# One-token attention from a key/value cache beside a small MLP: the unused matmuls of a step moved to its end and made 24, and the scores put behind all the transposes

## The chip, the cores and the metric

The kernel runs on one core of one Trainium2 chip. The metric is the device time in microseconds (us), taken as the median over several executions. Beside the times there is one profiled execution with its trace. A profile line names engines as PE (TensorE matmul), PEld (TensorE weight load), DVE (VectorE), ACT (ScalarE), POOL (GpSimd) and SP (SyncE, which issues the large transfers here).

## The reference

The inputs are bf16: two rows `x` of 512, key and value caches of shape 2 x 32 x 8192 x 128, and the weights of the projections and of the MLP.

```python
def _A_ref(x, k_cache, v_cache, wq, wo):      # H, Dh = 32, 128; Sq = 1
    q = (x @ wq).reshape(B, Sq, H, Dh).transpose(0, 2, 1, 3)
    scores = einsum("bhqd,bhkd->bhqk", q, k_cache) * (Dh ** -0.5)
    p = softmax(scores, axis=-1)
    o = einsum("bhqk,bhkd->bhqd", p, v_cache)
    return o.transpose(0, 2, 1, 3).reshape(B, Sq, H * Dh) @ wo

def _B_ref(x, w1, w2):
    return einsum("bsf,fd->bsd", maximum(einsum("bsd,df->bsf", x, w1), 0), w2)

xn = layernorm(x)
return x + _A_ref(xn, k_cache, v_cache, wq, wo) + _B_ref(xn, w1, w2)
```

There are 64 pairs of batch and head, and each has one query against 8192 keys. Every byte of the caches is read once and used once.

## The kernel before, in words

**Steps and tiles.** The 64 pairs are done four at a time (`U = 4`), so there are `NP = 16` steps. The keys of a step are one tile `ks` of 128 partitions by 32768 bf16: 32 partitions belong to one pair, and each partition holds 256 keys (`KB`) of 128 elements. The values of a step are a tile `vs` of the same form. There is one buffer of each: the next keys can be written over `ks` only when it has been read out, and the same holds for `vs`. The caches are 32 such tiles, which is 268 of the 280.5 MB that the profile counts as read.

**What TensorE does in a step.** The keys lie with the key number on the partitions, while the scores need the head's elements there. So the function `transposes(e)` (line 280) turns eight blocks of 128 x 128 through PSUM (`tp`, four buffers used in turn), and DVE or ACT copies each group of eight into one of 32 SBUF tiles `kT` (line 432, `kcopies`; twenty groups fall to DVE, twelve to ACT). `scores(e)` (line 287) multiplies the eight blocks of group `e` with the four queries `q4` into one PSUM area `Sc`. There are `NG = 32` groups. The first loop does `transposes(e)` and, from `e = LAG` on, `scores(e - LAG)` behind it; a second loop does the scores that are left. With `LAG = 28`, four score groups are mixed in: the order is T28 S0 T29 S1 T30 S2 T31 S3, then S4 to S31.

While the scores go on, DVE reduces them to a maximum (line 479), TensorE turns that (`turn`, line 299) and spreads it over the partitions (`spread`, line 305), and ACT takes the exponentials into `prm` (line 553). This is done for two halves of the scores. Then 256 matmuls of `vs` with `prm` (line 346) give the output `ot`; the last of them raises the semaphore `sW`.

**Unused matmuls.** At the head of each step stand `WARM = 16` matmuls of the identity with itself into the PSUM tile `ms` (line 313). Nobody reads their result. They wait for nothing. Behind them TensorE waits for the step's keys (`dK[0]`).

**Order of the transfers.** All large transfers are issued from SP's one queue, in a fixed order written by hand: keys of step 0, values of step 0, keys of step 1, values of step 1, and so on. Before it issues the keys of the next step, SP waits for the last transpose of this one (semaphore `pT[HG - 1]`); before it issues the next values it waits for `sW`:

```python
for t in range(NP):
    if t > 0:
        sp.wait_ge(pT[HG - 1], NH * t)
    load(ks, K_all, t, dK, 0 < t < NP - 1)
    if t == 0:
        sp.wait_ge(sQ, 2)
    else:
        sp.wait_ge(sW, t)
    load(vs, V_all, t, dV, t < NP - 1)
```

The first and the last step's keys and the last step's values are loaded in two halves with a semaphore each, the others whole. Ahead of the steps come the query projection (line 259); behind them the weights of the MLP and of the output projection are loaded over `ks` and used (lines 376 and 403). The output projection takes its weights in four pieces of 18, 8, 4 and 2 blocks.

**The loop on TensorE.** The steps are a run-time loop (`pe.Fori`), whose body is in the program once; a few registers (`reg`, `g`, `h`) hold the values that the semaphores are to reach and are advanced at its end. `reg` is 1 in the first step and 16 in the last.

Of the kernel before, what the change touches and what calls it, by code (L numbers as in the profile page):

```python
# [12 lines left out]
EG = 8  # L13
NG = 32
REP = 16
LAG = 28
TR = (21, 25)
BC = 32
WARM = 16
ON_ACT = (0, 3, 5)  # L20


# [1 line left out]
def kernel(  # L24
# [13 lines left out]
    P = 128  # L38
# [3 lines left out]

    Bsz, Sq, D = A_x.shape
    _, H, Sk, Dh = A_k_cache.shape
    Dff = B_w1.shape[1]
    assert Dh == P and D % P == 0 and Dff % P == 0 and Sk % HP == 0
# [4 lines left out]
    NP = N // U  # L51
# [17 lines left out]
    def sb(shape, dt, name):  # L69
        return ctx.enter_context(nc.sbuf_tensor(name, shape, dt))  # L70

    def ps(shape, dt, name):
        return ctx.enter_context(nc.psum_tensor(name, shape, dt))
# [14 lines left out]
    identb = sb([P, P], bf16, "identb")  # L88
# [41 lines left out]
    ms = ps([P, 512], f32, "ms")  # L130
# [80 lines left out]
    def advance(eng, regs):  # L211
        for r, step in zip(regs, (1, 2, 2) + (NH,) * NH):
            eng.reg_add(r, r, step)
# [35 lines left out]
    def _(pe):  # L249
        pe.wait_ge(sI, 1)  # L250
        pe.wait_ge(sV, 5)
        for kt in range(KT):
            i = pe.transpose(tpx[:, kt, :], xn[:, kt, :], identb[0:Bsz, 0:Bsz])
# [3 lines left out]
        for g in range(QG):  # L257
            for kt in range(KT):
                i = pe.matmul(  # L259
                    qp,  # L260
                    lhsT=xz[:, kt, Z - g * Bsz:Z - g * Bsz + QG * Bsz],
                    rhs=vs[:, (kt * QG + g) * 512:(kt * QG + g + 1) * 512],
                    start=(g == 0 and kt == 0),
                    stop=(g == QG - 1 and kt == KT - 1),
                )
        i.then_inc(sQ, 1)
        pe.wait_ge(sV, 7)
        for l in range(QH):
            i = pe.transpose(
                tpq[:, l, :], qs[:, l * Dh:(l + 1) * Dh], identb[0:QG * Bsz, 0:QG * Bsz]  # L270
            )
        i.then_inc(sQ, 1)

        def rep(ap, n):
            return ap.rearrange("p (o u) -> p o u", o=1).to_broadcast([P, n, U])

        def transposes(e):
            for i in range(EG):
                kk = e * EG + i
                t = pe.transpose(tp[e % 4][:, i, :], ks[:, kk * Dh:(kk + 1) * Dh], identb[:])  # L280
            t.then_inc(pT[e % HG], 1)

        def scores(e):
            for i in range(EG):
                kk = e * EG + i
                n = min(REP, BK - kk % BK)
                t = pe.matmul(  # L287
                    Sc[:, U * kk:U * (kk + n)],
                    lhsT=kT[e][:, i, :],
                    rhs=rep(q4[:], n),  # L290
                    start=True,
                    stop=True,
                )
            if e % (NG // 2) == NG // 2 - 1:
                t.then_inc(sS, 1)

        def turn(i):
            pe.wait_ge(sM, g[i])
            pe.transpose(  # L299
                trp[:, i * P:(i + 1) * P], mcol[:, i:i + 1], identb[:]  # L300
            ).then_inc(sT, 1)

        def spread(i):
            pe.wait_ge(sX, g[i])
            pe.matmul(  # L305
                bc[:, i, :], lhsT=onesb[:], rhs=mx[:, i, :], start=True, stop=True
            ).then_inc(sB, 1)

        regs = counters(pe, mybir.EngineType.PE)
        reg, g, h = regs[0], regs[1:3], regs[3:]  # L310
        with pe.Fori(16, NL + 1, 16) as n16:
            for i in range(WARM):
                pe.matmul(  # L313
                    ms[:], lhsT=identb[:],
                    rhs=identb[:].rearrange("p (o k) -> p o k", o=1).to_broadcast([P, 4, P]),
                    start=True, stop=True,
                )
            pe.wait_ge(dK[0], n16)
            pe.wait_ge(sQ1, reg)
            for e in range(NG):  # L320
                if e == NG // 2:
                    pe.wait_ge(dK[1], n16)
                if e >= 4:
                    pe.wait_ge(kR[(e - 4) % HG], h[(e - 4) // HG])
                transposes(e)
                if e >= LAG:
                    scores(e - LAG)
            for e in range(NG - LAG, NG):
                if e >= NG - 4:
                    pe.wait_ge(kR[e % HG], h[e // HG])  # L330
                scores(e)
                if e == TR[0]:
                    turn(0)
                if e == TR[1]:
                    spread(0)
            pe.wait_ge(sO, reg)
            for kk in range(KB):
                i, first = divmod(kk, KB // 2)
                if first == 0:
                    pe.wait_ge(sP, g[i])  # L340
                    if i == 0:
                        turn(1)
                    pe.wait_ge(dV[i], n16)
                if kk == BC:
                    spread(1)
                t = pe.matmul(  # L346
                    oh[:, i, :],
                    lhsT=vs[:, kk * Dh:(kk + 1) * Dh],
                    rhs=rep(prm[:, kk, :], REP),
                    start=(first == 0),  # L350
                    stop=(first == KB // 2 - 1),
                )
            t.then_inc(sW, 1)
            advance(pe, regs)

        pe.wait_ge(sI, 2 + U)
        dbp = Sc[:, 0:2 * N].rearrange("p (t u) -> p t u", u=U)
        for u in range(U):
            t = pe.matmul(  # L359
                dbp[:, :, u], lhsT=onesh[:, u, :], rhs=RS[:].rearrange("p i t -> p (i t)"),  # L360
                start=True, stop=True,
            )
        t.then_inc(sH, 1)
        for k in range(KT):
            pe.matmul(
                fin[:, k * Bsz:(k + 1) * Bsz],
                lhsT=xsb[:, k * P:(k + 1) * P],
                rhs=identb[0:Bsz, 0:Bsz],
                start=(k == 0),
                stop=False,  # L370
# [3 lines left out]
        for j in range(FJ):  # L374
            for kt in range(KT):
                i = pe.matmul(  # L376
                    hp[:, j, :],
                    lhsT=w1_v[:, kt, j, :],
                    rhs=xz[:, kt, Z:Z + Bsz],
                    start=(kt == 0),  # L380
                    stop=(kt == KT - 1),
                )
# [8 lines left out]
        for dq in range(DQ):  # L391
            t = pe.matmul(  # L392
                ox.rearrange("p (b j) -> p b j", b=Bsz),
                lhsT=sel[:, dq, :],
                rhs=Ob[:, :, dq * WJ:(dq + 1) * WJ],
                start=(dq == 0),
                stop=(dq == DQ - 1),
# [198 lines left out]
```

## Time and profile before

| | |
|---|---|
| median of 14 runs | 668.48 us |
| fastest and slowest of them | 663.64 and 676.11 us |
| the profiled execution, its own time | 673.97 us |
| its span, first to last instruction | 672.1 us |
| mean granted TensorE clock | 0.967 |
| PE, DVE, ACT busy | 587.2, 263.7 and 292.8 us |
| large transfers (SP's queue) | 280.50 MB, 97.6% of 16 engines' span |
| read from HBM | 417 GB/s over the span |

The profiled execution took 5.5 us more than the median, so it is one of the slower of its kind. The span leaves out 1.9 us of the execution's own time. "Busy" of PE counts overlapping pipelined matmuls and is no measure of how near it is to its peak. The row of the granted clock says what share of its full clock TensorE was given.

### The profile page before, as it was taken

The page shows a single profiled execution, that of the slowest core. Times are in us where ns is not written, and L with a number is a line of the kernel's source. Part 1 is how long each engine was busy: PE and PEld are TensorE (multiplying, and loading weights), DVE is VectorE, ACT ScalarE, POOL GpSimd, SP SyncE. Part 2 cuts the span into 40 slices and gives each one's busy share as a digit, 9 for nine tenths or more (in the row PEclk, how much of TensorE's full clock was granted, in tenths as well). Part 3 has the DMA queues.
Part 4 walks back from the last instruction along what each step waited for, and adds up shares of the span by engine and source line. Part 5 has one row for each costly group of instructions (what it writes and reads, how often), then busy time and mean ns, then how long its engine had stood idle before and what let it go on. Part 6 is the DMA issues. An engine that isn't in the chain of part 4 may idle for free.

```text
span 672.1 us, 27441 instructions
## 1 busy us (share of the span) xinstructions
PE 587.2 (87%) x12907; PEld 539.7 (80%) x12907; DVE 263.7 (39%) x503; ACT 292.8 (44%) x532; POOL 7.1 (1%) x30
## 2 busy tenths in 40 slices
PE   2986898979989998998989889897998979899997
PEld 0586787969878797987869688696987869698987
DVE  1350532607145160715417062260715317071721
ACT  1243543527244453725435363352636425373730
POOL 2000000000000000000000000000000000000000
PEclk9999999999889998999989989899989989999987
DMA  8999999999999999999999999999999999999995
GB/s 375 438 439 423 434 433 437 433 433 406 433 437 378 437 433 437 429 402 421 437 437 413 433 433 398 437 378 437 425 413 413 421 433 390 437 437 406 437 421 210
DMA packets 6079, 280.66 MB, mean 418 GB/s; under 512 B 690, under 2 KB 692, under 8 KB 948
## 3 DMA queue, kind: packets, MB, share of 16 engines
q1 hardware_dynamic: 6064, 280.50, 97.6%
q8 instruction: 8, 0.13, 0.1%
q14 instruction: 3, 0.02, 0.0%
q10 hardware_dynamic: 4, 0.00, 0.0%
HBM read 280.50 MB, written 0.00 MB: 417 GB/s over the span
## 4 chain that ended last, share of the span: by engine, by line
DMA 52%; PE 47%; DVE 1%; issue 0%; SPq 0%
DMA ks<-in_A_k_cache_dram 50%; PE tp L280 36%; PE Sc L287 4%; PE ot L346 3%; DMA vs<-in_A_wq_dram 2%; PE ot L259 1%; PE ms L313 1%; PE Sc L403 1%; PE ms L376 1%; DVE mcol L479 0%; PE Sc L359 0%; PE ms L299 0%; DVE qs L461 0%; PE ms L305 0%; PE ms L392 0%
## 5 line engine op out<-in xcount | busy, mean ns | idle before, releaser
L432 DVE COPY kT<-tp 128x1024 bf16<-128x1024 bf16 x320 | 211.1, 688 | 273.1 <-PE tp L280 267.4
L280 PE MATMUL tp<-identb,ks 128*128 128x128 bf16 x4096 | 248.7, 223 | 38.7 <-DMA ks<-in_A_k_cache_dram 38.7
L280 PEld LDWEIGHTS tp<-identb,ks 128*128 128x128 bf16 x4096 | 239.1, 100 | 46.1 <-DMA ks<-in_A_k_cache_dram 45.6
L432 ACT COPY kT<-tp 128x1024 bf16<-128x1024 bf16 x192 | 190.0, 1013 | 144.2 <-PE tp L280 142.1
L287 PE MATMUL Sc<-q,kT 128*128 128x64 bf16 (+8 forms) x4096 | 140.4, 191 | 2.1 <-issue 2.1
L346 PE MATMUL ot<-prm,vs 128*128 128x64 bf16 x4096 | 135.3, 195 | 4.3 <-issue 4.3
L346 PEld LDWEIGHTS ot<-prm,vs 128*128 128x128 bf16 x4096 | 131.2, 99 | 6.3 <-issue 4.5
L287 PEld LDWEIGHTS Sc<-q,kT 128*128 128x128 bf16 x4096 | 132.5, 97 | 3.5 <-issue 2.2
L553 ACT ACTIVATE prm<-Sc,nm 32x128 bf16<-32x128 f32 x128 | 69.0, 539 | 5.4
L479 DVE TENSOR_REDUCE mcol<-Sc 32x1 bf16<-32x128 f32 x128 | 37.1, 289 | 79.1 <-PE Sc L287 77.8
L548 ACT COPY nm<-ms 128x4 f32<-128x4 f32 x32 | 5.2, 163 | 134.7 <-PE ms L305 134.7
L313 PE MATMUL ms<-identb 128*128 128x512 bf16 x256 | 57.8, 379 | 0.6 <-issue 0.6
L313 PEld LDWEIGHTS ms<-identb 128*128 128x128 bf16 x256 | 23.9, 97 | 27.2 <-issue 0.6
L564 ACT COPY OTf<-ot 128x8 f32 x16 | 2.7, 166 | 75.8 <-PE ot L346 75.8
L553 ACT ACTIVATION_READ_ACCUMULATOR prm<-Sc,nm x128 | 32.1, 251 | 0.0
L299 PE MATMUL ms<-identb,mcol 128*1 128x128 bf16 x32 | 6.9, 217 | 22.1 <-DVE mcol L479 22.1
L432 ACT ACT_TABLE_LOAD x16 | 20.5, 1283 | 3.6 <-issue 3.6
L299 PEld LDWEIGHTS ms<-identb,mcol 128*1 128x1 bf16 x32 | 2.5, 79 | 23.9 <-issue 23.1
L259 PE MATMUL ot<-vs,xz 128*16 128x512 bf16 x32 | 9.1, 454 | 8.6 <-DMA vs<-in_A_wq_dram 8.6
L486 DVE TENSOR_REDUCE mx<-ms 1x4 bf16<-1x128 bf16 x32 | 8.9, 279 | 16.0 <-PE ms L299 16.0
L259 PEld LDWEIGHTS ot<-vs,xz 128*16 128x16 bf16 x32 | 3.3, 103 | 13.9 <-issue 11.4
L240 POOL COPY q<-qb 128x4 bf16<-128x4 bf16 x16 | 3.0, 188 | 603.6 <-PE Sc L287 555.6
(61 smaller groups left out, 46.9 us busy)
## 6 DMA issues: line engine op xcount, KB each, us to landing
ks<-in_A_k_cache_dram SPq DMA_DIRECT2D x4, 4096.0 KB, 22.7
vs<-in_A_v_cache_dram SPq DMA_DIRECT2D x2, 4096.0 KB, 21.6
vs<-in_A_wq_dram SPq DMA_DIRECT2D x1, 4096.0 KB, 12.1
ks<-in_B_w_dram SPq DMA_DIRECT2D x2, 1792.0 KB, 14.3
ks<-in_A_wo_dram SPq DMA_DIRECT2D x1, 2304.0 KB
ks<-in_A_wo_dram SPq DMA_DIRECT2D x1, 1024.0 KB, 23.3
ks<-in_A_wo_dram SPq DMA_DIRECT2D x1, 512.0 KB, 24.1
ks<-in_A_wo_dram SPq DMA_DIRECT2D x1, 256.0 KB, 24.2
```

The source lines that it names most:

```text
L259: i = pe.matmul(qp, lhsT=xz[:, kt, Z - g * Bsz:Z - g * Bsz + QG * Bsz], rhs=vs[:, (kt * QG + g) * 512:(kt * QG + g + 1) * 512], start=(g = ...
L280: t = pe.transpose(tp[e % 4][:, i, :], ks[:, kk * Dh:(kk + 1) * Dh], identb[:])
L287: t = pe.matmul(Sc[:, U * kk:U * (kk + n)], lhsT=kT[e][:, i, :], rhs=rep(q4[:], n), start=True, stop=True,)
L299: pe.transpose(trp[:, i * P:(i + 1) * P], mcol[:, i:i + 1], identb[:]).then_inc(sT, 1)
L313: pe.matmul(ms[:], lhsT=identb[:], rhs=identb[:].rearrange("p (o k) -> p o k", o=1).to_broadcast([P, 4, P]), start=True, stop=True,)
L346: t = pe.matmul(oh[:, i, :], lhsT=vs[:, kk * Dh:(kk + 1) * Dh], rhs=rep(prm[:, kk, :], REP), start=(first == 0), stop=(first == KB // 2 - 1),)
L376: i = pe.matmul(hp[:, j, :], lhsT=w1_v[:, kt, j, :], rhs=xz[:, kt, Z:Z + Bsz], start=(kt == 0), stop=(kt == KT - 1),)
L403: t = pe.matmul(fin[:, k * Bsz:(k + 1) * Bsz], lhsT=w[:, j, k * P:(k + 1) * P], rhs=x[:, j, :], start=False, stop=(last and k == KT - 1),)
L432: fn(kT[e][:], tp[e % 4][:]).then_inc(kR[e % HG], 1)
L479: m = v.tensor_reduce(out=mcol[own, i:i + 1], in_=S[own, i * KB // 2:(i + 1) * KB // 2, u], axis=AX.X, op=ALU.max,)
L486: v.tensor_reduce(out=mx[:, i, :], in_=trp[:, i * P:(i + 1) * P].rearrange("o (u m) -> o u m", u=U), axis=AX.X, op=ALU.max, negate=True,). ...
L553: x = a.activation(out=prm[own, k, u], in_=S[own, k, u], func=ACTF.Exp, bias=nm[own, i, u:u + 1], scale=1.0, accum_out=RS[own, i, bass.ds( ...
```

## The change

The 16 unused matmuls at the head of a step are taken out. At the end of the step, behind the last output matmul and its semaphore, stand 24 of them inside a branch on the register `reg`. The branch lets them run where `reg` is below 15, which is in the first fourteen steps; behind the last step but one and behind the last they are skipped. So none stands ahead of the first step, none ahead of the last, and 24 stand ahead of each of the others. `LAG` becomes 32: the first loop holds the 32 groups of transposes alone, and the second all 32 groups of scores.

```diff
-LAG = 28
+LAG = 32
 TR = (21, 25)
 BC = 32
-WARM = 16
+WARM = 24
...
         with pe.Fori(16, NL + 1, 16) as n16:
-            for i in range(WARM):
-                pe.matmul(
-                    ms[:], lhsT=identb[:],
-                    rhs=identb[:].rearrange("p (o k) -> p o k", o=1).to_broadcast([P, 4, P]),
-                    start=True, stop=True,
-                )
             pe.wait_ge(dK[0], n16)
             pe.wait_ge(sQ1, reg)
...
             t.then_inc(sW, 1)
+            with pe.If_lt(reg, NP - 1):
+                for i in range(WARM):
+                    pe.matmul(
+                        ms[:], lhsT=identb[:],
+                        rhs=identb[:].rearrange("p (o k) -> p o k", o=1).to_broadcast([P, 4, P]),
+                        start=True, stop=True,
+                    )
             advance(pe, regs)
```

## The prediction

> **What bounds the kernel now.** I read the page's busy slices first, then the DMA queue's own waits, the chain that ended last, and the timeline and stage windows around two neighbouring steps.
>
> ```profile
> PE   2986898979989998998989889897998979899997
> ...
> PEclk9999999999889998999989989899989989999987
> DMA  8999999999999999999999999999999999999995
> ...
> q1 hardware_dynamic: 6064, 280.50, 97.6%
> ...
> q8 instruction: 8, 0.13, 0.1%
> ```
>
> The transfers fill the span, so the time is 280.5 MB over the rate, plus whatever stops the transfers. PE's clock dips now and then. The queue's waits and the chain say what the transfers depend on:
>
> ```profile
> SPq L182 <- PE tp L280: 325.4, 15, 24.0
> SPq L182 <- PE ot L346: 262.6, 15, 23.7
> ...
> 87.85 23.45 DMA ks<-in_A_k_cache_dram
> ...
> 111.34 13.13 PE tp L280 x232
> ...
> 126.58 23.74 DMA ks<-in_A_k_cache_dram
> ...
> 150.37 14.75 PE tp L280 x232
> ...
> 167.23 24.63 DMA ks<-in_A_k_cache_dram
> ```
>
> The next keys (K) are issued when the last transpose is done; the values (V) of this step are then still landing. V's landing is its issue plus its time to landing in the DMA view: 104.97 + 25.7 = 130.7 us and 143.71 + 26.0 = 169.7. So in the first of these steps K is issued 126.58, which is 4.1 us ahead of V's landing, and lands 150.32 - 130.7 = 19.6 us after it. In the second it is issued at 167.23, only 2.5 us ahead, and lands 191.86 - 169.7 = 22.2 us after V. I did this for the thirteen whole K loads from 87.85 on. Seven leads are 4.0 to 4.4 us, with intervals 19.3, 19.6, 19.7, 19.3, 19.4, 20.0 and 20.5. Six are 2.4 to 2.8 us (issues at 167.2, 208.5, 364.2, 405.2, 445.8, 565.9), with intervals 22.2, 19.3, 21.7, 21.2, 20.9 and 20.4. A load without trouble takes 19.35 us. The late six cost 125.7 - 6 x 19.35 = 9.6 us, the other seven 137.8 - 7 x 19.35 = 2.4.
>
> ```profile
> vs<-in_A_v_cache_dram SPq DMA_DIRECT2D x1, 25.7
> ...
> vs<-in_A_v_cache_dram SPq DMA_DIRECT2D x1, 26.0
> ...
> 143.60:150.40 6.80, 3.62 (x20) 1.48 (x18) 0.00 (x0) 1.45 (x2) 0.00 (x0) 1.00 0.93 405
> 150.40:153.80 3.40, 3.40 (x33) 3.40 (x34) 1.36 (x2) 1.01 (x1) 0.00 (x0) 0.50 1.11 482
> ...
> 111.30:114.70 3.40, 3.36 (x61) 3.37 (x61) 2.00 (x4) 2.38 (x3) 0.00 (x0) 1.00 1.11 482
> ```
>
> These stage windows say why six were late (the third figure from the end is the clock). From V's issue to K's landing PE has 3.6 us of unused matmuls and then nothing; in the first 3.4 us of the transposes the clock is 0.50 with 33 matmuls, against 1.00 and 61 in the other step. The transposes then take 14.75 us instead of 13.13, and K's issue moves back by 1.6 us. The idle time before the transposes is 1.6 to 3.9 us over the steps; the cold starts follow 2.55 us and more, none a smaller one, though some gaps near 3 us stay warm.
>
> **The change, part by part.** The sum is made against the profiled execution's own 673.97 us (span 672.1 and 1.9 around it), which is 5.5 above the median.
>
> *24 instead of 16 unused matmuls, steps 1 to 14.* The 16 take 3.61 us, so one takes 3.61 / 16 = 0.22 and 24 take about 5.3. They start where they did: the end of a step and the head of the next are one stretch of PE's queue, behind the semaphore that releases V. From the last output matmul to K's landing there are 6.3 us in a usual step (104.97 to 111.29) and 4.7 to 5.1 where the output matmuls met a half clock (225.63 to 230.63). The gap shrinks from some 2.7 us to 1.0, and at its longest (541.63 to 549.02, 7.4 us) to 2.1, under the 2.55 from which I saw cold starts. In the short steps the block runs past K's landing by up to 0.6 us. It takes DVE, ACT and DMA nothing; what hides it is the wait for K, and where that cover is gone each us delays the transposes and K's issue one for one.
>
> *All scores behind all transposes.* Three score groups, 3 x 0.25 us in the chain, leave the stretch ahead of the last transpose: K's issue comes 0.75 us earlier, while the scores end as before and V's issue does not move. What has to keep up is the copy out of PSUM: DVE does five of each eight groups in 3.37 us and waits 0.20 for PE, so it follows at PE's pace for four more groups; the former breaks were spare. I cost it at 0, at most 0.2.
>
> Both together: the lead of K over V's landing is 4.1 + 0.75 = 4.85 us in a usual step and 4.85 - 0.6 = 4.25 where the block overruns. No step should be left at 2.4 to 2.8, so the 9.6 us go. The seven early steps' 2.4 us may go in part; I leave them in, and put them into the range.
>
> A rule of the Trainium skill speaks against putting every score behind the transposes. "TensorE: Matmul & The Clock Gate", Part 4, says that transposes do not count as busy work and that the full clock does not engage for them. By the rule the unbroken stretch would run at half the clock: 256 transposes in some 27 us instead of 14.4, an estimate, so about 12 us more per step. The row says otherwise: 232 unbroken transposes took 13.13 us, 57 ns each, at a clock of 1.00. I take the row.
>
> *None ahead of the first step.* The block there took 3.6 us of the chain at 23.86. The transposes start that much earlier, but K of step 1 was issued at 42.54, 10.6 us ahead of V's landing at 53.2. Worth 0; if the first transposes ran cold, the same lead covers it.
>
> *None ahead of the last step.* Here PE is the bound:
>
> ```profile
> 621.13 3.50 PE ms L313 x16
> 624.63 12.95 PE tp L280 x232
> ...
> 658.20 0.89 PE Sc L359 x8
> ...
> 663.83 5.02 PE Sc L403 x184
> ```
>
> All of PE behind it comes 3.5 us earlier. Two transfers can take that back. The last keys' second half lands near 628.3 (the two issues at 604.03 land after 19.2 us in the middle, 9.7 us apart); the first half of the transposes from 621.2 ends at 628.4, so it costs nothing. The last piece of the output weights, issued near 642.0, lands 24.2 later, at 666.2; eight matmuls at 5.02 / 184 = 27 ns follow, to 666.4, where the line now ends at 668.85. So 3.5 shrinks to 2.4 us.
>
> *The branch.* By the rows of the loop line, a branch of TensorE's sequencer takes 69 to 226 ns. Sixteen of them, each under 0.3 us, stand behind V's release and ahead of the unused matmuls or an empty wait: 0 in the middle. Skipped, one is on the path ahead of the last step and one behind it: at most 0.4 together. A rule speaks against it: "Runtime: NRT & Kernel Launch", Instruction fetch mechanics, says that a taken branch out of a two-page window makes the engine stall for a fetch. The trace has such stalls in the first pass of the body:
>
> ```profile
> 63.31 3.21 PE L346 MATMUL ot<-prm,vs 128*128 128x64 bf16 x101 [3.11 <-issue]
> ```
>
> They are 1.2 to 3.1 us each. By the rule the two taken skips cost up to 6.2 us, one of them on the path of the end, and the 2.4 would be gone. But every step already ends with a taken branch over the whole body, and the page has 8 instruction packets in all with no such stall after the first pass; a skip over 48 instructions is shorter. I take 0, and keep 3 for the range.
>
> Sum: 673.97 - 9.6 - 2.4 = 662.0. What is left holds no late K, so it should not depend on how many of them a run drew; against the median it is 6.5 lower. The fastest of the 14, 663.64, which can have had little of this loss, gives 663.64 - 2.4 = 661.2. I take 661.5, with 659 (the other 2.4 us gone too) to 664.5 (the fetch) as this case's own range.
>
> **Rivals.** *The late issue is not the cause* (the slow loads are the memory's doing, and the late transposes only stand beside them). For it: one late step, 208.5, lost nothing, and two early ones, 484.8 and 524.5, lost 0.7 and 1.1. Against: five of six late ones lost 1.0 to 2.8. Then the end's 2.4 us remain: 668.48 - 2.4 = 666.1, no change by the bound below.
>
> *The block becomes the bound ahead of the transposes,* the slower side. In steps with a half clock in the output matmuls the 24 already overrun; if the half clock falls on them, 3.4 us of it adds 1.7. It decides where the overrun passes about 2 us, since 4.85 - 2 is the late lead of 2.8. If all 14 steps got there, each would lose 1.6 (9.6 / 6): 14 x 1.6 - 9.6 - 2.4 = 10.4 more, 673.97 + 10.4 = 684 in that run and some 679 against the median. Against it: the half clocks before 256 and 495 lay early in the output matmuls and were over by the block.
>
> *The body no longer fits what the sequencer keeps.* It grows by 16 instructions and a branch. The stalls came every 256 instructions; the last was followed by 101 matmuls, some 203 of 256 with weight loads, so about 30 stay free. Were it wrong, each step would pay 6.4 us as the first did, for 15 steps up to 96. Very unlikely.
>
> **How the numbers follow.** The forecast has 0.76; the late issue not being the cause 0.12; the overrun 0.07; the fetch 0.02; mishaps in between, 664 to 666, 0.03. What a measurement of this kernel can tell from no change is about 0.5%, 3.3 us, so faster is under 665.1. Faster 0.79, same 0.12, slower 0.09. The range 659 to 667 takes in the forecast and the 666.1; outside are the slower cases, 0.09, and some tail on both sides.
>
> **What would show it.** Right: no clock of 0.50 at the start of the transposes; K's issue 14.5 us behind its landing instead of 15.3 or 16.9; intervals from V's to K's landing of 19.3 to 19.7 throughout; no line 313 between the last two steps; the last weights waited for by line 403. The half clocks in the output matmuls should stay. Wrong: transposes waiting for the unused matmuls by over 2 us; K's intervals still over 20 with leads near 4.8; instruction packets in the middle of the span.

## The result

The changed kernel takes 659.35 us (median of 10 runs, 658.82 to 662.31) against 668.83 for the kernel before (47 runs, 663.64 to 676.42). The ratio is 0.9879, with a 95% interval of 0.9858 to 0.9901. The forecast was 661.5 in a range of 659 to 667; the result lies near its lower end. The profiled execution took 659.67 us, its span is 657.9.

The page of the changed kernel, the rows that were shown of the kernel before:

```profile
span 657.9 us, 27617 instructions
...
PEclk9895999999899999999989999999999999999996
DMA  9999999999999999999999999999999999999996
...
q1 hardware_dynamic: 6064, 280.50, 98.9%
...
q8 instruction: 8, 0.13, 0.1%
```

The clock has lost most of its dips; the transfers fill 98.9% of a shorter span. The queue's waits (who waited for whom, total us, times, longest):

```profile
SPq L182 <- PE tp L280: 298.9, 15, 20.5
SPq L182 <- PE ot L340: 275.9, 15, 26.7
```

The chain that ended last, over two steps (start us, us, what):

```profile
397.59 24.16 DMA ks<-in_A_k_cache_dram
...
421.79 14.48 PE tp L280 x256
...
436.29 24.16 DMA ks<-in_A_k_cache_dram
```

SP still waits for the same two, less for the transposes and more for the outputs. From the fourth step on all steps but the last look much the same: the transposes take 14.5 us in one piece, and K (the next keys) is issued 14.5 to 14.7 us after the landing of the last. Here it is issued at 397.59, 4.80 us ahead of the landing of V (the step's values) at 402.39 in the trace's landing events, and lands 19.35 us after V. Of the thirteen whole K loads from that of step 2 on, twelve landed 19.35 to 19.37 us after V and one 19.68. The shortest lead is 4.34 us.

Stage windows of one step (window, its length, PE, PEld, DVE, ACT, POOL busy; then clock, DMA share, GB/s):

```profile
376.80:383.10 6.30, 5.14 (x25) 2.17 (x23) 0.00 (x0) 1.45 (x2) 0.00 (x0) 1.00 1.03 447
383.10:386.50 3.40, 3.40 (x61) 3.40 (x62) 2.05 (x4) 2.42 (x3) 0.00 (x0) 1.00 0.98 424
```

From V's issue to K's landing TensorE is now busy for 5.1 of 6.3 us, and the transposes start at a clock of 1.00. The end, in the chain:

```profile
626.80 27.41 DMA ks<-in_A_wo_dram
654.21 0.05 issue
654.26 0.39 PE Sc L404 x8
...
654.89 0.28 PE tp L424
```

The last weights and eight matmuls set the end, where 184 matmuls in one piece had done so before.

**Where the time came from.** The keys of the last step but one landed at 588.75 us before and land at 576.56 now: 12.2 us come from ahead of it, nearly all from the thirteen K loads, which lost 12.2 us in all before and lose 0.4 now. From there to the end of the span it was 83.35 us and is 81.3: 2.0 from the last step. Together 14.2 of the 14.3 us between the two profiled executions. The medians differ by 9.5 only, since the profiled execution of the kernel before was one of its slower ones.

### The profile page after: what moved, and what is told of

It is laid out like the page before. It is cut to its first block, busy times and chain, and to the rows that moved or that the text cites. A ratio compares the mean times of both kernels' runs of the same rounds, so it can differ in the third digit from the quotient of the medians.

```text
span 657.9 us, 27617 instructions
## 1 busy us (share of the span) xinstructions
PE 599.4 (91%) x12987; PEld 542.0 (82%) x12987; DVE 261.8 (40%) x503; ACT 290.7 (44%) x532; POOL 7.1 (1%) x30
## 3 DMA queue, kind: packets, MB, share of 16 engines
q1 hardware_dynamic: 6064, 280.50, 98.9%
## 4 chain that ended last, share of the span: by engine, by line
PE 54%; DMA 43%; issue 1%; DVE 1%; ACT 0%; SPq 0%; POOL 0%; ACTq 0%; DVEq 0%; POOLq 0%
DMA ks<-in_A_k_cache_dram 37%; PE tp L280 35%; PE ot L340 7%; PE Sc L287 6%; DMA ks<-in_A_wo_dram 4%; PE ms L350 3%; DMA vs<-in_A_wq_dram 2%; PE ot L259 2%; DVE mcol L480 1%; PE ms L299 0%; SPq L198 0%; ACT L433 0%; PE ms L305 0%; ACT kT L433 0%; DVE qs L462 0%
## 5 line engine op out<-in xcount | busy, mean ns | idle before, releaser
L280 PEld LDWEIGHTS tp<-identb,ks 128*128 128x128 bf16 x4096 | 230.7, 98 | 19.7 <-DMA ks<-in_A_k_cache_dram 16.9
L280 PE MATMUL tp<-identb,ks 128*128 128x128 bf16 x4096 | 233.2, 220 | 13.5 <-DMA ks<-in_A_k_cache_dram 11.5
L287 PE MATMUL Sc<-q,kT 128*128 128x64 bf16 (+8 forms) x4096 | 134.2, 192 | 1.0 <-issue 1.0
L287 PEld LDWEIGHTS Sc<-q,kT 128*128 128x128 bf16 x4096 | 129.6, 98 | 6.0 <-issue 4.8
L350 PE MATMUL ms<-identb 128*128 128x512 bf16 x336 | 74.8, 379 | 0.0
L350 PEld LDWEIGHTS ms<-identb 128*128 128x128 bf16 x336 | 31.8, 98 | 36.4
```

The costliest lines, as they stand in the source:

```text
L287: t = pe.matmul(Sc[:, U * kk:U * (kk + n)], lhsT=kT[e][:, i, :], rhs=rep(q4[:], n), start=True, stop=True,)
L350: pe.matmul(ms[:], lhsT=identb[:], rhs=identb[:].rearrange("p (o k) -> p o k", o=1).to_broadcast([P, 4, P]), start=True, stop=True,)
```

## The experiments

The theory: what costs time is K issued too late ahead of V's landing, and the half clock at the start of the transposes matters only because it makes K late. The first rival: the slow loads are the memory's doing. The second: the half clock costs time of its own. "Lead" is the time from K's issue to V's landing; "loss" is what the time from V's landing to K's exceeds 19.35 us. Each ratio is to the kernel before, run beside it; a trace is that of one run.

### One part at a time

**LAG alone**

```diff
-LAG = 28
+LAG = 32      # kernel before, all else as it was
```

> The kernel before with LAG = 32 alone: 16 unused matmuls at the head of every step, as before. Theory (a late issue of the next keys makes their load slow, and a half clock at the start of the transposes is what makes it late): the half clocks stay in about six steps, K's lead over V's landing is 4.85 us in a step at full clock and 4.85 - 1.6 = 3.2 in one with a half clock. The loss in those falls from 1.6 us to about half, the small losses of the others go: about 665 us (668.8 - 3.5). Rival (the slow loads are the memory's doing, whatever the issue): 668.8. Second rival (the half clock costs its own 1.6 us on the path, six times, whatever the lead): also 668.

Measured: 667.81 us, ratio 0.9982 (0.9946 to 1.0019): no gain that can be told. The chain of its profile:

```profile
403.46 24.15 DMA ks<-in_A_k_cache_dram
427.66 16.11 PE tp L280 x256
443.79 24.09 DMA ks<-in_A_k_cache_dram
467.93 14.48 PE tp L280 x256
```

Four of thirteen steps still began at half clock, with transposes of some 16.1 us in place of 14.48. Their leads were 3.16 to 3.20 us and they lost 1.0 to 1.8 us each. The expectation gave them half of 1.6: the lead was right, the loss at it was not. The profiled run, 672.58 us, is the slowest of the ten. Its K loads lost 6.1 us in all, half of the 12.2 before; 2.4 more were lost by V of the second step (below).

**24 unused matmuls and the skip, LAG as before**

```diff
-LAG = 32      # changed kernel
+LAG = 28
```

> The changed kernel with LAG = 28: 24 unused matmuls at the end, none ahead of the first and last step, four score groups still mixed into the transposes. Theory: no half clock at the start of the transposes, leads of 4.1 us, 3.6 where the unused matmuls run past K's landing; the small losses of the early steps stay, 2 to 3 us in all: 659.4 + 2.5 = 661.9. If LAG carries most of the gain: 665 or more. Rival (memory): only the last step's gain, 666.

Measured: 665.21 us, ratio 0.9950 (0.9915 to 0.9984), its runs from 659.90 to 669.91. In the profiled run (663.64) only one step of thirteen was at half clock. Most leads were 4.04 to 4.17 us, and of those two lost 0.8 and 1.0; one of 3.61 lost 1.9. In all its K loads lost 4.5 us. The expected 661.9 was too low: nine of the ten runs took more. That the loss at such leads comes and goes from run to run would fit the spread, but only one run has a trace.

**The skip alone**

```diff
-LAG = 32      # changed kernel
+LAG = 28
-WARM = 24
+WARM = 16
```

> The changed kernel with LAG = 28 and 16 unused matmuls: only the place and the skip ahead of the first and last step remain of the change. Theory: the half clocks and late issues stay, the end is 2.3 us shorter: 668.8 - 2.3 = 666.5. If the branch cost a fetch on the path: 668 to 669.

Measured: 667.48 us, ratio 0.9999 (0.9968 to 1.0029). The 2.3 us cannot be told in the time. In its trace they are there at the end: the span ends 3.7 us after the landing of the last weights, as in the changed kernel, against 5.9 before.

**16 in place of 24, the rest as changed**

```diff
-WARM = 24     # changed kernel
+WARM = 16
```

> The changed kernel with 16 unused matmuls in place of 24, all else as changed (LAG 32, none ahead of the first and last step). Theory: the idle time ahead of the transposes is again near 2.7 us, half clocks come in about four of 13 steps, each with a lead of 3.2 us and a loss of 1.5 us as in the kernel with LAG = 32 alone: 659.4 + 6 = 665.4. If the number of unused matmuls does not matter: 659.4.

Measured: 664.07 us, ratio 0.9941 (0.9904 to 0.9978). Five of the thirteen steps began at half clock again, with transposes of 15.9 to 17.2 us in place of 14.5, and the leads behind them were 2.1 to 3.4 us. This took back about half of the gain. In the profiled run (666.80) the K loads lost 3.6 us in all, and V of the second step 2.9 (below).

**No skip: 24 at the head of every step**

```diff
-WARM = 16     # kernel before
+WARM = 24
-LAG = 28
+LAG = 32
```

> The kernel before with LAG = 32 and 24 unused matmuls at the head of every step, the first and the last too: the changed kernel without its branch. Theory: the loads are as fast as in the changed kernel; in the last step TensorE starts its transposes 24 x 0.216 = 5.2 us later, and the end is again set by it and not by the last weights. In the kernel with LAG = 32 and 16 at the head the last transfer landed 6.8 us before the span's end, against 3.7 in the changed kernel; with 24 it should be 6.8 + 8 x 0.216 = 8.5: 659.4 + 4.8 = 664.2. If the skip is worth nothing: 659.4.

Measured: 664.09 us, ratio 0.9925 (0.9885 to 0.9966), as expected in size but not in its parts. The chain of its end:

```profile
642.48 6.87 PE ot L346 x224
...
654.98 5.01 PE Sc L403 x184
```

TensorE sets the end again: the span ends 6.65 us after the last weights landed (656.59), against 3.7 with the skip. That is 3.0 us, not the 4.8 expected; another 2.3 were lost in the second step, where V's issue came late (below), so that the sum fits by luck.

Alone, LAG gave 0.2% and the skip 0.0. The 24 were run only together with the skip (0.5%), not by themselves. Taken out of the whole, each part costs 4.7 to 5.9 us between the medians, or 0.5 to 0.7% between the ratios, which is little more than their intervals can tell. So they are not three gains that add up: the loads are quick only when every step keeps its distance, and the end shows it only if TensorE is out of its way.

### The lead by itself

**Later issue at full clock**

```diff
-LAG = 32      # changed kernel
+LAG = 24      # and 16 in a second run
```

> The changed kernel with LAG = 24: eight score groups mixed into the transposes, so the last transpose and with it K's issue is 7 x 0.25 = 1.75 us later in every step, at full clock. Theory (the lead alone decides): leads of 4.85 - 1.75 = 3.1 us in every step, each losing about 1.5 us as the steps with 3.2 did: 659.4 + 13 x 1.5 = 679. Rival (a slow load needs the half clock beside it, or is the memory's doing): 659 to 660.

> The changed kernel with LAG = 16: sixteen score groups mixed in, K's issue 15 x 0.25 = 3.75 us later. Theory: leads of 1.1 us in every step at full clock, losing 1.5 to 2.5 us each: 680 to 692. Rival (half clock or memory): 659 to 660.

Measured: 678.53 us with 24, ratio 1.0184 (1.0103 to 1.0265); 689.11 us with 16, ratio 1.0321 (1.0226 to 1.0417). Nothing else differs from the changed kernel but where score groups stand; the work is the same. The condition "at full clock in every step" was not met: seven of the thirteen K loads with 16, and three with 24, follow a step that began at half clock. With 16, chain rows at two neighbouring K loads, each with the transposes that follow it; the second load comes behind transposes at full clock (7.77 us for 136, against 9.39 in the next step):

```profile
419.91 21.79 DMA ks<-in_A_k_cache_dram
441.74 7.77 PE tp L280 x136
...
459.91 21.79 DMA ks<-in_A_k_cache_dram
481.74 9.39 PE tp L280 x136
```

Both K loads land 21.79 us after their issue. V's issues before them, 392.71 and 435.84, landed after 26.7 and 25.2 us in the DMA view, at 419.4 and 461.0. The first K was issued 0.5 us behind V's landing and lost 3.0 us (441.7 - 419.4 - 19.35); the second 1.1 us ahead, and lost 1.4. So 2.4 us pass beside the 19.35 of transfer when the issue comes this late (21.79 - 19.35). The rival "memory" is out: the loads are slow where the issue is late, with 16 in every one of the thirteen steps. With 24, eight leads were 3.0 to 3.4 us, and these loads lost 0 to 1.5, 0.6 in the mean and not the 1.5 expected. The largest losses, 3.1 and 3.5, stand at leads of 1.8 and 1.7, each behind a step that began at half clock. The K loads lost 11.7 us in all in that run (675.34), so that 678.53 against the expected 679 is in part luck.

Over nine profiled executions (the kernel before, the changed one, the five of the parts and these two), the 117 K loads of steps 2 to 14 (counted from 0) by their lead:

| lead, us | loads | mean loss, us | largest | behind a step that began at half clock |
|---|---|---|---|---|
| 4.5 and more | 42 | 0.02 | 0.4 | 0 |
| 4.0 to 4.5 | 26 | 0.2 | 1.1 | 0 |
| 2.3 to 4.0 | 31 | 0.9 | 2.8 | 20 |
| 1.5 to 2.3 | 4 | 2.4 | 3.5 | 4 |
| 1.1 to 1.4 | 7 | 1.4 | 1.5 | 1 |
| -0.5 (behind it) | 7 | 3.0 | 3.2 | 7 |

The change moves nearly all steps from the second and third row into the first. Late issue and half clock mostly come together here, so the second rival needs the cases where they part. Six loads at leads of 1.1 to 1.2 follow steps at full clock and lost 1.3 to 1.5 us each. With 40 unused matmuls (below) no step from the second on begins at half clock, and twelve K loads with leads of -1.1 to 1.1 lost 1.4 to 3.8. The other way round, the first step of the changed kernel had a half clock near the start of its transposes, which took 16.08 us in place of 14.48:

```profile
25.44 16.08 PE tp L280 x256
```

Yet the K load issued behind them was 12.0 us ahead and lost 0.07. So a late issue costs without a half clock, and this half clock cost the transfers nothing with an early issue. The lead is not the whole account of a loss, though: at 2.3 to 4.0 us the 20 loads behind a half clock lost 1.1 us in the mean and the other 11 lost 0.6. Whether a half clock adds to the loss at such leads stays open.

**Early issue without touching TensorE's work**

```diff
 # kernel before
-            if t > 0:
-                sp.wait_ge(pT[HG - 1], NH * t)
-            load(ks, K_all, t, dK, 0 < t < NP - 1)
+            for i in range(2):
+                if t > 0:
+                    sp.wait_ge(pT[HG - 1], NH * (t - 1) + NH // 2 * (i + 1))
+                c = slice(i * SLOT // 2, (i + 1) * SLOT // 2)
+                sp.dma_start(ks[:, c], K_all[t * P:(t + 1) * P, c]).then_inc(dK[i], 16)
...
-            if 0 < t < NP - 1:
-                g.wait_ge(dK[0], 16 * (t + 1)).then_inc(dK[1], 16)
```

> The kernel before with the keys of every step loaded in two halves: the first half is issued when the first 16 groups of transposes are done, the second after the last. Unused matmuls and LAG as before. Theory: the half clocks stay where they were, yet the next keys' first half is now issued over 10 us ahead of the landing of the values, so no load is slow: only the end differs from the changed kernel, 659.4 + 2.3 = 661.7. Rival (memory): 668.8. Second rival (the half clock itself costs): 668 too.

Measured: 659.48 us, ratio 0.9872 (0.9818 to 0.9927): the whole gain with LAG at 28, 16 unused matmuls at the head of every step and no branch. SP's timeline:

```profile
413.05 0.33 SPq L182 DMA_DIRECT2D vs<-in_A_v_cache_dram  x1
423.75 8.21 SPq L189 DMA_DIRECT2D ks<-in_A_k_cache_dram  x2
```

And a row of its chain:

```profile
413.05 28.17 DMA vs<-in_A_v_cache_dram
```

V lands at 441.2; the first half of K is issued at 423.75 and the second by 431.96 (the merged row covers both), so even the second is over 9 us ahead. In every step the second half of K lands 19.4 us after V, and no load is slow. Two things came out otherwise than expected. The half clocks did not stay at the start of the transposes: the first half of K is there before TensorE comes to it, so no idle time stands ahead of the transposes, and the half clocks moved to the output matmuls. And the end needed no skip: TensorE runs half a tile ahead and is out of the way in the last step too. So this run shows that an early issue is enough; it does not show that a half clock at the start of the transposes would cost nothing by itself.

**The halves with no unused matmuls**

```diff
-WARM = 24     # changed kernel with the halves above
+WARM = 0      # and no branch
```

> The changed kernel with the keys loaded in two halves, the first issued when 16 groups of transposes are done, and with no unused matmuls at all. Theory: the transposes start at half clock in most steps, the lead is some 10 us anyway, no load is slow: 659.5, as with the halves in the kernel before. Rival (a half clock costs its own time): 13 x 1.6 = 21 more, 680.

Measured: 659.32 us, ratio 0.9881 (0.9811 to 0.9951). The halves need neither the unused matmuls nor the branch. Here too the half clocks of the later steps fell into the output matmuls, 13 of them. One such stage window, of the halves in the kernel before:

```profile
404.90:408.30 3.40, 3.40 (x68) 3.40 (x66) 0.00 (x0) 2.28 (x9) 0.00 (x0) 0.50 1.07 463
```

Without the unused matmuls the mean clock is 0.933 over the span, against 0.971 in the changed kernel, and the time is the same: the clock lost there, off the path, cost nothing. Neither version beats the changed kernel by more than the intervals can tell.

### The unused block as the bound

```diff
-WARM = 24     # changed kernel
+WARM = 40     # and 48 in a second run
```

> The changed kernel with 40 unused matmuls in place of 24: they take 16 x 0.216 = 3.5 us more and run past the landing of K by some 2.3 us in a usual step. Theory (the unused block becomes the bound ahead of the transposes, the slower rival of the prediction made true): no half clock at the start of the transposes, K's lead 4.85 - 2.3 = 2.5 us in every step, each K load losing 0 to 2.8 us, 1.4 in the mean of such leads so far: 659.4 + 13 x 1.4 = 678. If the matmuls are hidden: 659.4.

Measured: 691.65 us, ratio 1.0330 (1.0277 to 1.0383), 13 us more than expected. The chain between two starts of the block holds no transfer at all:

```profile
394.89 8.63 PE ms L350 x40
403.53 14.29 PE tp L280 x256
417.82 5.39 PE Sc L287 x176
...
437.09 8.63 PE ms L350 x40
```

The K loads did lose, 0.7 to 3.8 us each, but TensorE did not wait for them: the transposes began 2.6 to 6.0 us after K's landing. Its own cycle had become the longer one (42.2 us here, with a half clock in its output matmuls, and 40.8 in the steps without). From K's landing to the last output matmul it takes 32.4 us, with 8.63 for the block 41.0, against 2 x 19.35 = 38.7 for the two transfers. Fourteen times 2.3 us are 32, and 659.35 + 32 = 691, an estimate that meets the measured time.

> The changed kernel with 48 unused matmuls: the loop's body grows by 48 more instructions and, by the count from the stalls of the first step (203 of 256 used before, 16 and a few branch instructions added by the change), passes the next multiple of 256 instructions. If the sequencer then loses the start of the body: instruction packets in every step and stalls of some 6 us in each on top of the overrun: 740 or more. If it keeps the body: only the overrun of 4 us, a lead of 0.8 us, a loss of 2.55 - 0.8 = 1.75 us per step: 659.4 + 13 x 1.75 = 682.

Measured: 981.42 us, ratio 1.4652 (1.4561 to 1.4744). A row of the page:

```profile
q8 instruction: 144, 2.36, 0.9%
```

Two of the timeline around the loop's start (start us, us, engine and line; in brackets the idle time before it, and why):

```profile
314.13 10.52 PE L350 MATMUL ms<-identb 128*128 128x512 bf16 x48
328.57 5.39 PE L280 MATMUL tp<-identb,ks 128*128 128x128 bf16 x49 [3.91 <-issue]
```

There are 144 instruction packets in place of 8, some nine in each pass, and TensorE stands idle several times per step with no releaser that the profile shows ("issue"). With 40 there were still 8 packets. The eight matmuls between, 16 instructions, cost 290 us, of which 14 x 8 x 0.216 = 24 are their own time.

## Why the prediction was right

**The late issue was the cost, and it went.** Late K loads were to give 9.6 us, and the lead to be 4.85 in a usual step. It is 4.80, and 4.34 to 4.38 behind the two steps where the unused block overran most (forecast 4.25). The K loads gave some 11.8 in the profiled pair. What was mis-sized is mainly one term: "the seven early steps' 2.4 us may go in part; I leave them in". They went too, since a lead of 4.0 to 4.5 still loses something now and then (0.2 us in the mean) and one of 4.5 and more hardly does (0.02). With them the sum would have been 662.0 - 2.4 = 659.6, against 659.67 in the profiled execution. The cause given for it, a late issue, is shown by the sweep of LAG and by the halves; they rule out the rival "the late issue is not the cause".

**The half clocks at the transposes went.** The gap was to shrink to 1.0 us: it is 1.05 to 1.2 in ten steps, and in the four others the block runs past K's landing by up to 0.6, as forecast. (Of the 4.7 to 5.1 us that the prediction gave to the short steps of the kernel before, the 4.7 stands in no row: its shortest are 5.0 and 5.1.) At the start of the transposes the clock was full in all of steps 1 to 15, and half clocks stayed in the output matmuls of steps 1, 3 and 7; the one early dip at 26 us is in the first step, whose lead covers it.

**All scores behind all transposes cost nothing elsewhere.** 256 unbroken transposes took 14.48 us at a clock of 1.00, so the row and not the rule of the Trainium skill ("TensorE: Matmul & The Clock Gate", Part 4) held for the unbroken stretch, and the copies kept up. Nor did transposes that began at a clock of 0.50 stay there: in the kernel before they took 14.75 us for 232 in place of 13.13.

**The last step gave 2.0 of the 2.4 forecast.** The span now ends 3.7 us after the landing of the last weights in place of 5.9. That is 2.2; the weights themselves landed 18.95 us after the last V in place of 18.44, and the transfers ahead of them gave back 0.3. One reading in the working was wrong as well. The transposes started at 609.23, right behind the outputs, but then stood still, as the timeline shows:

```profile
609.23 1.95 PE L280 MATMUL tp<-identb,ks 128*128 128x128 bf16 x32 [0.28 <-issue]
609.45 1.28 ACT L433 ACT_TABLE_LOAD   x1 [0.23 <-issue]
...
611.81 1.40 PE L280 MATMUL tp<-identb,ks 128*128 128x128 bf16 x22 [0.64 <-ACT kT L433]
```

"It costs nothing" had overlooked ACT: 32 transposes fill the four PSUM buffers, and the copy of the first group waits behind ACT's table load, 1.28 us, which the unused matmuls had covered. In the last step the transposes took 15.3 us in place of 14.5, so about 0.8 of the 3.5 us was lost there; the wait for the last weights hid it.

**The branch.** It takes 77 ns where the matmuls run and 208 where they are skipped, and no instruction packet came with it, so the forecast of 0 held. The rule of the Trainium skill ("Runtime: NRT & Kernel Launch", Instruction fetch mechanics) that a taken branch out of a two-page window stalls, is hardly tested by this skip, which passes over 48 instructions. What speaks against it is the branch back over the whole body of some 1,600 instructions, taken 15 times while all packets but two, which come behind the loop, lie in the first pass. With 48 unused matmuls packets and stalls came in every pass. That the body then passed a multiple of 256 instructions, as was expected, fits this; only the two sizes, 40 and 48, show where it begins.

**The rivals' prices were too low.** For the block as the bound, 1.6 us per late K was the wrong term; at an overrun of 2.3 us it was TensorE's cycle that counted (41.0 us against 38.7). For the body that no longer fits, 96 us had been worked out from the first pass; it was 322 in all (981.4 - 659.35), of which the longer cycle of 48 matmuls explains 14 x (32.4 + 48 x 0.216 - 38.7), some 57.

## What to carry to other kernels

When one queue feeds a kernel that is bound by its transfers, look at how far ahead of the running transfer's landing the next one is issued; here 4.5 us was enough, and an issue some 2 us later cost up to 2.8 us a load. Issue the next transfer for half a buffer as soon as that half is free: it did here what 24 idle matmuls, a branch and a new order did together, and it does not depend on a clock. Parts that each gain nothing alone can be worth 1.2% together when they depend on each other, so test them by taking one out as well as by adding one.

## What the runs showed of the hardware

A lead that is just too short can cost more than a later issue: at 1.1 to 1.4 us ahead the loads lost 1.3 to 1.5 us each, at 1.5 to 4.0 anything from 0 to 3.5. In the trace of the kernel before, the K load issued at 167.23 us found the first of the 16 DMA engines done with V at 167.5 and came to its own first packet at 168.2; most of its first packets took 2.6 to 3.4 us in place of 2.42, and one engine started 1.3 us behind the rest and took 3.98. What makes these packets slow was not tried.

The second step has the same trouble with its V. In the first pass of the loop six of the eight instruction packets come beside the full stream of transfers (between 31.9 and 70.3 us in the changed kernel), and there TensorE stood for 3.52 us before line 299. In four of the nine executions V of the second step was issued only 2.1 to 2.6 us ahead of K's landing and lost 2.3 to 2.9 us; in the other five the lead was 4.2 to 6.8 and they lost 0.1 at most. That may be why some runs of the changed kernel took 661.5 to 662.3 us; it was not tried. The row of the changed kernel's timeline:

```profile
51.57 0.26 PE L299 MATMUL ms<-identb,mcol 128*1 128x128 bf16 x1 [3.52 <-issue]
```
